# Sparse attention and a gated MLP in one kernel: the scores of the first chunk between its transposes, small copies moved between engines, and one unit's output transposed on TensorE

## The chip, the cores and the metric

The kernel runs on one core of a Trainium2 chip. It is one program with five instruction queues: TensorE (PE, its weight loads shown apart as PEld), VectorE (DVE), ScalarE (ACT), GpSimd (POOL) and SyncE (SP, which here only issues DMAs). The engines work through their own queues in order and wait for each other by semaphores. The metric is the device time of one execution in microseconds (us); lower is better.

## The reference

Attention with 4 batches, 8 heads, 768 positions and a head width of 64, all in float32, then an MLP. Heads 0, 2 and 6 are full causal heads ("retrieval"); the other five see only the first 4 positions and a window of 64.

```python
scores = scale * q @ k.transpose(0, 1, 3, 2)
causal = rel >= 0                          # rel = query position - key position
stream = causal & ((pos_k < n_sink) | (rel < window))     # n_sink 4, window 64
a = softmax(where(causal if retrieval[head] else stream, scores, -1e9))
x = (a @ v).transpose(0, 2, 1, 3).reshape(3072, 512)      # heads side by side
h = x @ w_in                               # w_in 512 x 2048
out = (h * sigmoid(beta * h)) @ w_out      # w_out 2048 x 512
```

## The kernel before, in words

**Units and chunks.** The work is cut into 32 units. A unit is one pair of heads for one half (384 rows) of one batch; four units make a chunk (384 rows of all 8 heads), and there are 8 chunks. Units 0 to 3 are chunk 0 (batch 0, first half), units 4 to 7 chunk 1 (batch 1, first half), units 8 to 11 chunk 2 (batch 0, second half), and so on.

**Steps of a unit.** `steps_T` transposes keys and queries on TensorE (line 350), the results are copied out of PSUM to `KT` (VectorE, line 351) and to the two halves of `QTD` (line 356). `sinks_of` makes `KO` on GpSimd: a copy of the key blocks with the sink columns put in (lines 333 and 334). `steps_QK` multiplies (line 415), for units below 8 adds the mask by a second matmul (line 421), and ScalarE takes the exponential into `es` (line 424). The scores of a unit come in three or more fills; a fill that holds a window block with sinks reads `KO`. `values` casts v into `VX` (`cast_v`, line 275) and copies the masked blocks into `VO` on GpSimd (lines 285 and 286). `steps_PV` multiplies into `po` (line 459), and VectorE normalises into `x` (lines 462 and 464). `x` is transposed into `xT` either on TensorE (`steps_X`, line 491, copied out of PSUM at line 493) or by a DMA (`x_by_dma`, line 475, from SP's queue; units 8 to 29).

**The MLP.** `steps_G1` is a product of four matmuls with `w_in` (line 510), a tanh on ScalarE (line 513) and the gate on VectorE (line 516): 16 such groups for a chunk, which need all four `xT` of the chunk. `steps_G2` is the product with `w_out` (line 534), copied out by ScalarE (line 538) and stored. These groups fill TensorE between the attention steps.

**Loads.** For chunks 0 to 2, q and k come as float32 by SP (`load_qk`, line 119: two pairs of heads at a time) and are cast to bfloat16 into `qkb` by `cast` (line 269; the engine is chosen by the caller); v comes by SP too (`load_v`, line 132). `held=True` puts a small memset on GpSimd ahead of the load, so that the load is issued only when GpSimd's queue gets there. `load_w_in` (line 140) and `load_w_out` (line 144) are DMAs from GpSimd's queue that cast on the way. From chunk 3 on the rows of q and k are loaded and cast by GpSimd's DMAs (lines 303 and 308) into the former staging buffers (`rows_queries` clears one of them first, a memset of 128 x 1536, line 232), and DMA transposes on SP's queue make `KT` (line 319) and `QTD` (line 322).

**The order.** The order on every engine is the order of the calls in the program. The part for chunks 0 and 1 (lines 653 to 736, the "ramp" here) is written out by hand. From unit 8 on, a loop over slots `t` lays scores of unit t, values of unit t - 1 and a fixed number of MLP groups beside each other; `later(delay, f)` places work of the other engines by a running estimate of TensorE's time. PSUM holds two buffers for transposes (`tp`), two for scores (`sp`), three shared ones (`mm`) and one for `po`.

Of the kernel before, what the change touches and what calls it, by code (L numbers as in the profile page):

```python
# [17 lines left out]
def kernel(  # L18
# [13 lines left out]
    nc = tc.nc  # L32
# [66 lines left out]
    st_u = {}  # L99
# [23 lines left out]
    def load_v(c, held=False, tiles=range(HT)):  # L123
        b, h2 = chunks[c]
        if tiles[0] == 0:
            staged["v", c] = stage.tile([128, HT, H, D], F32, name="vs")
        vs = staged["v", c]
        if held:
            nc.gpsimd.memset(vs[:, :, 0, 0:1], 0.0)
        for t in tiles:  # L130
            r = h2 * HALF + t * 128
            nc.sync.dma_start(out=vs[:, t], in_=v[b, :, r:r + 128, :].rearrange("h p d -> p h d"))
# [5 lines left out]
    def load_w_in(i):  # L138
        f = slice(i * 512, (i + 1) * 512)
        nc.gpsimd.dma_start(out=w_in_sb[:, :, f], in_=moe_w_in.rearrange("(mo mi) f -> mi mo f", mi=128)[:, :, f])  # L140
# [54 lines left out]
    def negatives():  # L195
        nc.vector.tensor_scalar(out=Mc, in0=Nc, scalar1=0.0, scalar2=None, op0=ALU.is_ge)
        for i, m in enumerate([M0, Mo, Md, Mo, Md]):
            nc.vector.tensor_scalar(out=Ns[:, i * 128:(i + 1) * 128], in0=m, scalar1=-1.0, scalar2=-NEG, op0=ALU.add, op1=ALU.mult)
# [72 lines left out]
    def cast_v(u):  # L271
        b, h2, p = units[u]
        c = u // NPAIR
        copy = nc.scalar.copy if u in (1, 3) else nc.vector.tensor_copy if 8 <= u < 16 else nc.gpsimd.tensor_copy
        copy(out=VX[b % 2, p][:, h2 * HT:(h2 + 1) * HT, :, 0:D], in_=staged["v", c][:, :, 2 * p:2 * p + 2, :])  # L275

    def values(u):
# [64 lines left out]
    def steps_T(u):  # L342
        b, h2, p = units[u]
        s = st_u.setdefault(u, {})

        def go():
            tk, tq = tile_t(), tile_t()
            for i, tp in ((1, tk), (0, tq)):
                for t in range(HT):
                    nc.tensor.transpose(tp[:, t, :], s["qkb"][:, i, t].rearrange("p h d -> p (h d)"), ident)  # L350
            nc.vector.tensor_copy(out=KT[b % 2, p][:, h2 * HALF:(h2 + 1) * HALF].rearrange("p (j t) -> p j t", t=HT),  # L351
                                  in_=tk.rearrange("p t j -> p j t"))
            s["QT"] = QT = QTB[u % 3]
            for hh in range(2):
                copy = nc.vector.tensor_copy if hh and u not in (1, 4) else nc.scalar.copy
                copy(out=QT[hh][half(hh), :].rearrange("p (j t) -> p j t", t=HT),  # L356
                     in_=tq[half(hh)].rearrange("p t j -> p j t"))

            if u >= 8:
                s["values"] = later(1500, lambda: values(u))  # L360
            s["sinks"] = later(600, lambda: sinks_of(u))
        return [(350, go)]
# [79 lines left out]
    def steps_PV(u):  # L442
        b, h2, p = units[u]
        s = st_u.setdefault(u, {})

        def head(hh, qi, last):
            def go():
                for f in s["masks"] + [s["values"]]:
                    f()
                if "po" not in s:  # L450
                    if u < 8 and u % 2:
                        po = ps_m.tile([128, 512], F32, name="mm") if u < 4 else ps_s.tile([128, 512], F32, name="sp")
                        s["po"] = po[:, 0:HT * 2 * (D + 1)].rearrange("p (t h d) -> p t h d", t=HT, h=2)
                    else:
                        s["po"] = ps_o.tile([128, HT, 2, D + 1], F32, name="po")
                po = s["po"]
                lst = s["blocks"][hh][qi]
                for j, (e, val) in enumerate(lst):
                    nc.tensor.matmul(po[:, qi, hh, :], e, val, start=(j == 0), stop=(j == len(lst) - 1))  # L459
                if last:  # L460
                    rec = att.tile([128, HT, 2, 1], F32, name="rec")
                    nc.vector.reciprocal(rec, po[:, :, :, D:D + 1])
                    x = att.tile([128, HT, 2, D], BF16, name="x")
                    nc.vector.tensor_mul(x, po[:, :, :, 0:D], rec.to_broadcast([128, HT, 2, D]))  # L464
                    s["x"] = x
                    if 8 <= u < NU - 2:
                        later(700, lambda: x_by_dma(u))
            return (len(s["blocks"][hh][qi]) * 38, go)
        return [head(hh, qi, hh == 1 and qi == HT - 1) for qi in range(HT) for hh in range(2)]
# [11 lines left out]
    def steps_X(u):  # L481
        b, h2, p = units[u]
        s = st_u.setdefault(u, {})

        def go():
            c = u // NPAIR
            if c not in xT:
                xT[c] = moe.tile([128, MO, HALF], BF16, name="xT", bufs=3)
            tp = tile_t()
            for t in range(HT):  # L490
                nc.tensor.transpose(tp[:, t, :], s["x"][:, t].rearrange("p h d -> p (h d)"), ident)
            copy = nc.scalar.copy if u < 8 else nc.vector.tensor_copy
            copy(out=xT[c][:, p, :], in_=tp.rearrange("p t j -> p (t j)"))
            avail.add((c, p))
            since[c] = clock[0]
            del st_u[u]
        return [(170, go)]
# [125 lines left out]
    def transposes_of(u):  # L623
        step(steps_T(u)[0])

    def run(steps):
        for x in steps:
            step(x)
# [19 lines left out]
    def cast_dp(u):  # L648
        cast(u, "k", dve)
        cast(u, "q")  # L650


    cast_dp(0)
    load_v(0, held=True)
    transposes_of(0)
    cast_dp(1)
    transposes_of(1)
    negatives()
    st_u[0]["sinks"]()
    st_u[1]["sinks"]()  # L660
    load_w_in(0)
    load_qk(1, 0, held=True)
    cast_dp(2)
    cast_dp(3)
    run(steps_QK(0))
    transposes_of(2)
    run(steps_QK(1))
    transposes_of(3)
    run(steps_QK(2))
    run(steps_QK(3))  # L670
    st_u[2]["sinks"]()
    load_qk(1, 1, held=True)
    rows_queries(1, "s1")
    st_u[3]["sinks"]()
    load_v(1, held=True)
    step((100, beta_go))
    for u in range(4):
        values(u)
    cast(4, "kq", nc.scalar.copy)
    cast(5, "q")  # L680
    load_w_in(1)

# [7 lines left out]
    cast(5, "k", dve)  # L690
    qk = steps_QK(4)
    step(qk[0])
    run(steps_PV(3))
    step(qk[1])
    step(steps_X(2)[0])
    transposes_of(5)
    step(qk[2])
    step(steps_X(3)[0])
    load_w_in(2)
    cast_dp(6)  # L700
    run(steps_QK(5))
    ms(1)
    transposes_of(6)
    ms(1)
    cast_dp(7)
    run(steps_QK(6))
    load_w_in(3)
    transposes_of(7)
    ms(1)
    run(steps_QK(7))  # L710
    ms(1)
    for u in range(4, 8):
        st_u[u]["sinks"]()
    values(4)
    values(5)
    load_w_out(0)
    load_w_out(1)
    values(6)
# [35 lines left out]
    for t in range(8, NU + 2):  # L754
        if t == 8:
            cast_dp(9)
        if t + 2 < 12:
            cast_dp(t + 2)
        if t == 11:
            rows_queries(0, "s0")  # L760
        if t == 12:
            masks_late(0)

        if t < 11:
            some = rows3[6:] if t == 8 else []
        elif t < 14:
            some = load_rows(4)[3 * (t - 11):3 * (t - 10)]
        else:
            c = (t + 6) // NPAIR
            i = (t + 6) % NPAIR  # L770
            some = load_rows(c)[i * 2 + (i > 1):i * 2 + 2 + (i > 0)] if c < NCHUNK else []
        for i, f in enumerate(some):
            later(1000 + 1500 * i, f)
        c, i = (t + 4) // NPAIR, (t + 4) % NPAIR
        if t >= 12 and c < NCHUNK and i < HT:
            later(2500, lambda c=c, i=i: load_v(c, tiles=[i]))
        if t == 9:
            transposes_dma(3, "k")
        if t == 10:
            transposes_dma(3, "q")  # L780
        if t >= 14 and t % NPAIR == 2 and t // NPAIR + 1 < NCHUNK:
            transposes_dma(t // NPAIR + 1)
        if 12 <= t + 1 < NU:
            sinks_at(t + 1, 1000)
            values_at(t + 1, 3000)
        qk = steps_QK(t) if t < NU else []
        pv = steps_PV(t - 1) if 8 <= t - 1 < NU else []
        xx = steps_X(t - 2) if t >= NU else []
        tr = steps_T(t + 1) if t + 1 < 12 else []

        A = qk[:2] + xx
        qk = qk[2:]
        n = max(len(qk), len(pv))
        for i in range(n):
            A += pv[i:i + 1] + qk[i:i + 1] + (tr if i == 0 else [])
        nm = nm_of.get(t, 7)
        if t >= NU:
            ms(3)
            nm -= 3
        slot(A, nm)  # L800
# [41 lines left out]
```

## Time and profile before

| | us |
|---|---|
| median of 3 runs (lowest, highest) | 245.78 (244.87, 248.98) |
| the profiled execution, its own time | 245.14 |
| its span, first to last instruction | 243.4 |
| PE busy | 228.4 (94%) |
| DVE / ACT / POOL busy | 147.3 / 160.9 / 102.8 |
| bytes moved by DMA | 33.85 MB |

The profiled execution lies 0.64 us under the median. Its span leaves out 1.74 us around the first and last instruction. A row of the timeline gives start, duration, engine, line, operation and what it writes and reads; a row of the waits gives who waited for whom, total, times and longest, all in us. A DMA row in the list of issues ends with the time from issue to landing. In the row of the windows the number behind the engines' columns is the granted clock of TensorE, 1.00 being full speed. Matmuls are pipelined, so durations of neighbours overlap; distances between starts are the better measure there.

### The profile page before, as it was taken

How to read it: one execution, taken by the hardware profiler on the slowest of the kernel's cores; microseconds unless marked ns; L12 is line 12 of the kernel's file. 1: busy time of each engine (PE TensorE's matmuls, PEld its weight loads, DVE VectorE, ACT ScalarE, POOL GpSimd, SP SyncE). 2: the span in 40 equal slices, each digit the busy share in tenths (PEclk: the TensorE clock that was granted, in tenths of full speed). 3: DMA queues.
4: the chain of work that ended last, by engine and by line, in shares of the span. 5: the costliest groups of instructions: out<-in, count | busy, mean ns of one | idle time of the engine just before them, and what ended most of it. 6: DMA issues, size and time to landing. Idle time of an engine off the chain costs nothing.

```text
span 243.4 us, 5238 instructions
## 1 busy us (share of the span) xinstructions
PE 228.4 (94%) x1901; PEld 138.4 (57%) x1901; DVE 147.3 (61%) x379; ACT 160.9 (66%) x312; POOL 102.8 (42%) x247
## 2 busy tenths in 40 slices
PE   7687999999999979799999999999999999999993
PEld 3476665555565656556655666566655666455541
DVE  4747668885787559855774577447762766345400
ACT  2598877875757769746775568667884877256510
POOL 6667399011839964297228823950380000000000
PEclk9799999999999999999999999999999999999999
DMA  6999989999989999999989996989421100201112
GB/s 205 192 280 221 180 133 207 213 157 251 189 171 155 183 184 170 153 110 163 147 197 125 168 197 139 147 163 148 103 62 59 60 18 0 79 10 46 43 46 86
DMA packets 103658, 33.85 MB, mean 139 GB/s; under 512 B 90304, under 2 KB 100560, under 8 KB 103632
## 3 DMA queue, kind: packets, MB, share of 16 engines
q1 hardware_dynamic: 67392, 24.98, 49.0%
q0 software_dynamic: 35664, 8.13, 38.7%
q10 hardware_dynamic: 576, 0.40, 0.5%
q8 instruction: 15, 0.25, 0.4%
q14 instruction: 11, 0.09, 0.1%
HBM read 27.27 MB, written 6.29 MB: 138 GB/s over the span
## 4 chain that ended last, share of the span: by engine, by line
PE 79%; ACT 5%; DVE 5%; DMA 4%; POOL 4%; issue 2%; POOLq 0%; ACTq 0%
PE mm L510 30%; PE tp L534 25%; PE sp L415 8%; PE mm L534 7%; PE po L459 4%; ACT es L424 2%; DMA QTD<-s 2%; DMA xT<-x 2%; PE mm L167 2%; DVE gT L516 1%; PE tp L350 1%; ACT QTD L356 1%; DVE x L464 1%; POOL VX L275 1%; ACT osb L538 1%
## 5 line engine op out<-in xcount | busy, mean ns | idle before, releaser
L510 PE MATMUL mm<-xT,w_in_sb 128*128 128x384 bf16 x512 | 98.1, 326 | 1.7 <-DMA xT<-x 1.4
L513 ACT ACTIVATE th<-mm,beta_h 128x384 f32<-128x384 f32 x128 | 74.5, 582 | 27.2 <-PE mm L510 22.5
L516 DVE SCALAR_TENSOR_TENSOR gT<-th,mm 128x384 bf16<-128x384 f32 x128 | 69.8, 551 | 31.0 <-ACT th L513 28.0
L534 PE MATMUL tp<-w_out_sb,gT 128*128 128x512 bf16 x288 | 70.7, 379 | 0.5 <-ACT osb L538 0.5
L510 PEld LDWEIGHTS <-w_in_sb 128*128 128x128 bf16 x512 | 46.2, 97 | 26.3 <-issue 1.6
L534 PEld LDWEIGHTS <-gT 128*128 128x128 bf16 x384 | 34.9, 98 | 30.7 <-issue 0.6
L415 PE MATMUL sp<-QTD,KT 128*128 128x128 bf16 (+2 forms) x261 | 46.4, 244 | 2.7 <-DMA QTD<-s 1.3
L424 ACT ACTIVATE esL<-sp 128x384 bf16<-128x384 f32 x72 | 37.7, 542 | 15.3 <-PE sp L415 15.1
L424 ACT ACTIVATE es<-sp 128x512 bf16<-128x512 f32 (+1 forms) x56 | 30.8, 561 | 7.5 <-PE sp L415 6.9
L415 PEld LDWEIGHTS <-KT 128*128 128x128 bf16 x272 | 25.1, 99 | 12.9 <-issue 4.2
L534 PE MATMUL mm<-w_out_sb,gT 128*128 128x512 bf16 x96 | 24.1, 379 | 0.0
L275 POOL CAST VX<-vs 128x384 bf16<-128x384 f32 x22 | 11.3, 516 | 30.2 <-issue 16.1
L308 POOL DMA_DIRECT2D s<-in_q_dram x30 | 22.3, 751 | 2.2 <-issue 1.7
L333 POOL COPY KO<-KT 128x128 bf16<-128x128 bf16 (+1 forms) x32 | 13.0, 406 | 22.3 <-DVE KT L351 17.2
L538 ACT ACTIVATE osb<-tp 128x512 f32<-128x512 f32 x18 | 10.8, 597 | 14.7 <-PE tp L534 14.4
L459 PEld LDWEIGHTS <-es 128*128 128x128 bf16 x220 | 14.1, 98 | 8.9 <-issue 1.5
L459 PEld LDWEIGHTS <-esL 128*128 128x128 bf16 x252 | 14.7, 98 | 7.7 <-DVE x L464 0.5
L431 DVE TENSOR_TENSOR es<-es,Mh 128x512 bf16<-128x512 bf16 (+2 forms) x30 | 12.9, 431 | 8.3 <-ACT es L424 8.2
L436 DVE TENSOR_TENSOR esL<-esL,Mc 128x128 bf16<-128x128 bf16 x36 | 9.1, 252 | 12.2 <-ACT esL L424 12.2
L459 PE MATMUL po<-VX,esL 128*128 128x65 bf16 x216 | 16.3, 193 | 0.1
L464 DVE TENSOR_TENSOR x<-po,rec 128x384 bf16<-128x384 f32 x28 | 15.6, 557 | 1.0
L415 PE MATMUL sp<-QTD,KO 128*128 128x128 bf16 x79 | 14.8, 220 | 0.0
(85 smaller groups left out, 214.8 us busy)
## 6 DMA issues: line engine op xcount, KB each, us to landing
vs<-in_v_dram SPq DMA_DIRECT2D x24, 256.0 KB, 5.0
out_dram<-osb SPq DMA_DIRECT2D x24, 256.0 KB, 2.5
w_in_sb<-in_moe_w_in_dram POOLq DMA_DIRECT2D x4, 512.0 KB, 5.9
w_out_sb<-in_moe_w_out_dram POOLq DMA_DIRECT2D x4, 512.0 KB, 9.0
s<-in_k_dram SPq DMA_DIRECT2D x5, 384.0 KB, 5.9
s<-in_q_dram SPq DMA_DIRECT2D x5, 384.0 KB, 6.7
s<-in_k_dram POOLq DMA_DIRECT2D x15, 128.0 KB, 5.6
s<-in_q_dram POOLq DMA_DIRECT2D x30, 64.0 KB, 4.0
```

The lines of the kernel that those rows point to most:

```text
L275: copy(out=VX[b % 2, p][:, h2 * HT:(h2 + 1) * HT, :, 0:D], in_=staged["v", c][:, :, 2 * p:2 * p + 2, :])
L308: nc.gpsimd.dma_start(out=ROWS[c % 2, "q"][:, t, :, 3 * D * hh:3 * D * hh + D], in_=q[b, hh:H:2, r:r + 128, :].rearrange("h p d -> p h d"))
L333: nc.gpsimd.tensor_copy(out=ko[:, ka - 1:kz - 1, :], in_=kt[:, ka * 128:kz * 128].rearrange("p (a j) -> p a j", a=n))
L415: nc.tensor.matmul(sp[:, (i - lo) * 128:(j - lo) * 128], lst[i][1], s["QT"][lst[i][0]][:, q0 * 128:(q0 + j - i) * 128], start=True, stop=n ...
L424: nc.scalar.activation(out=es[:, lo * 128:hi * 128], in_=sp[:, 0:w], func=ACTF.Exp, scale=scale)
L459: nc.tensor.matmul(po[:, qi, hh, :], e, val, start=(j == 0), stop=(j == len(lst) - 1))
L464: nc.vector.tensor_mul(x, po[:, :, :, 0:D], rec.to_broadcast([128, HT, 2, D]))
L510: nc.tensor.matmul(hp[:, 0:HALF], w_in_sb[:, mo, fi * 128:(fi + 1) * 128], xT[c][:, mo, :], start=(mo == 0), stop=(mo == MO - 1))
L513: nc.scalar.activation(out=th, in_=hp[:, 0:HALF], func=ACTF.Tanh, scale=beta_h[:, fi:fi + 1])
L516: nc.vector.scalar_tensor_tensor(out=gTs[c][:, fi, :], in0=th, scalar=1.0, in1=hp[:, 0:HALF], op0=ALU.add, op1=ALU.mult)
L534: nc.tensor.matmul(op, gTs[c][:, fi, ns * 128:(ns + 1) * 128], w_out_sb[:, fi, :], start=(fi == 0), stop=(fi == FO - 1))
L538: nc.scalar.activation(out=osb, in_=op, func=ACTF.Copy, scale=0.5)
```

## The change

- **Ramp, chunk 0.** The first fill of a unit's scores is put ahead of the transposes of the next unit (before, both transposes of units 0 and 1 came first and then whole units of scores). `negatives()` (six small VectorE operations that make the additive masks) goes ahead of the first `KT` copy. k of unit 1 is cast on ScalarE instead of VectorE. `load_qk(1, 1)` is released right behind `load_qk(1, 0)`.
- **Copies.** `VX` of units 1 and 3 goes from ScalarE to VectorE, one `QTD` half of unit 1 from ScalarE to VectorE, `xT` of units 0 and 1 from ScalarE to VectorE. q and k of unit 4 were both cast on ScalarE; now k is cast on VectorE between the two `VX` copies and q on GpSimd between `values(1)` and `values(2)`.
- **GpSimd's queue.** The casts of units 6 and 7 are split and drawn forward. `values(4)`, the load of the last quarter of `w_in`, `values(5)` and the memset of `rows_queries(1, "s1")` move from behind the scores of unit 7 (and, the memset, from ahead of v of chunk 1) to directly behind the scores of unit 5, and so ahead of `KO` of unit 6.
- **Unit 11.** Its `x` is transposed on TensorE in slot 13 instead of by DMA. The DMA transposes of the keys of chunk 4 are issued at slot 13 instead of 14, those of its queries at slot 14 as before, and the row loads for chunks 3 and 4 are placed closer together.

```diff
-        copy = nc.scalar.copy if u in (1, 3) else nc.vector.tensor_copy if 8 <= u < 16 else nc.gpsimd.tensor_copy
+        copy = nc.vector.tensor_copy if u in (1, 3) or 8 <= u < 16 else nc.gpsimd.tensor_copy
...
-                copy = nc.vector.tensor_copy if hh and u not in (1, 4) else nc.scalar.copy
+                copy = nc.vector.tensor_copy if hh and u != 4 else nc.scalar.copy
...
-                    if 8 <= u < NU - 2:
+                    if 8 <= u < NU - 2 and u != 11:
                         later(700, lambda: x_by_dma(u))
...
-            copy = nc.scalar.copy if u < 8 else nc.vector.tensor_copy
+            copy = nc.scalar.copy if 2 <= u < 8 else nc.vector.tensor_copy
...
     cast_dp(0)
     load_v(0, held=True)
+    negatives()
     transposes_of(0)
-    cast_dp(1)
+    st_u[0]["sinks"]()
+    cast(1, "k", act)
+    cast(1, "q")
+    qk = steps_QK(0)
+    step(qk[0])
     transposes_of(1)
-    negatives()
-    st_u[0]["sinks"]()
+    step(qk[1])
+    step(qk[2])
     st_u[1]["sinks"]()
+    cast_dp(2)
     load_w_in(0)
     load_qk(1, 0, held=True)
-    cast_dp(2)
+    load_qk(1, 1, held=True)
     cast_dp(3)
-    run(steps_QK(0))
+    qk = steps_QK(1)
+    step(qk[0])
     transposes_of(2)
-    run(steps_QK(1))
+    step(qk[1])
+    step(qk[2])
+    qk = steps_QK(2)
+    step(qk[0])
     transposes_of(3)
-    run(steps_QK(2))
+    step(qk[1])
+    step(qk[2])
     run(steps_QK(3))
     st_u[2]["sinks"]()
-    load_qk(1, 1, held=True)
-    rows_queries(1, "s1")
     st_u[3]["sinks"]()
     load_v(1, held=True)
     step((100, beta_go))
-    for u in range(4):
-        values(u)
-    cast(4, "kq", nc.scalar.copy)
+    values(0)
+    values(1)
+    cast_dp(4)
+    values(2)
+    values(3)
     cast(5, "q")
     load_w_in(1)
...
     step(qk[0])
+    cast(6, "q")
+    load_w_in(2)
     run(steps_PV(3))
...
-    load_w_in(2)
-    cast_dp(6)
+    cast(7, "q")
+    cast(6, "k", dve)
     run(steps_QK(5))
+    values(4)
+    load_w_in(3)
+    values(5)
+    rows_queries(1, "s1")
     ms(1)
     transposes_of(6)
     ms(1)
-    cast_dp(7)
+    cast(7, "k", dve)
     run(steps_QK(6))
-    load_w_in(3)
...
-    values(4)
-    values(5)
     load_w_out(0)
...
-        if t < 11:
-            some = rows3[6:] if t == 8 else []
-        elif t < 14:
-            some = load_rows(4)[3 * (t - 11):3 * (t - 10)]
+        if t < 14:
+            some = rows3[6:] if t == 8 else load_rows(4)[3 * (t - 11):3 * (t - 10)] if t > 10 else []
...
-            later(1000 + 1500 * i, f)
+            later((1000 if t != 13 else 200) + (1500 if t > 13 else 1000) * i, f)
...
+        if t == 13:
+            transposes_dma(4, "k")
+        if t == 14:
+            transposes_dma(4, "q")
-        if t >= 14 and t % NPAIR == 2 and t // NPAIR + 1 < NCHUNK:
+        if t > 14 and t % NPAIR == 2 and t // NPAIR + 1 < NCHUNK:
             transposes_dma(t // NPAIR + 1)
...
-        xx = steps_X(t - 2) if t >= NU else []
+        xx = steps_X(t - 2) if t == 13 or t >= NU else []
```

More of the change, by code (lines that the diff above doesn't have):

```diff
@@ L650, in cast_dp @@
         cast(u, "q")
+    act = nc.scalar.copy
     cast_dp(0)
     load_v(0, held=True)
+    negatives()
     transposes_of(0)
-    cast_dp(1)
+    st_u[0]["sinks"]()
[3 more added lines that the diff above has]
+    step(qk[0])
     transposes_of(1)
-    negatives()
-    st_u[0]["sinks"]()
+    step(qk[1])
+    step(qk[2])
     st_u[1]["sinks"]()
+    cast_dp(2)
     load_w_in(0)
     load_qk(1, 0, held=True)
-    cast_dp(2)
+    load_qk(1, 1, held=True)
     cast_dp(3)
-    run(steps_QK(0))
+    qk = steps_QK(1)
+    step(qk[0])
     transposes_of(2)
-    run(steps_QK(1))
+    step(qk[1])
+    step(qk[2])
+    qk = steps_QK(2)
+    step(qk[0])
     transposes_of(3)
-    run(steps_QK(2))
+    step(qk[1])
+    step(qk[2])
     run(steps_QK(3))
     st_u[2]["sinks"]()
-    load_qk(1, 1, held=True)
-    rows_queries(1, "s1")
     st_u[3]["sinks"]()
```

## The prediction

> **What bounds the kernel now.** I read the page first, then what TensorE waits for.
>
> ```profile
> span 243.4 us, 5238 instructions
> ...
> PE   7687999999999979799999999999999999999993
> ...
> PEclk9799999999999999999999999999999999999999
> ...
> PE 79%; ACT 5%; DVE 5%; DMA 4%; POOL 4%; issue 2%; POOLq 0%; ACTq 0%
> ```
>
> TensorE is nine tenths busy from slice 6 on, so whatever comes late there moves the end, and work hidden elsewhere does not. Its idle time is in the first six slices (0 to 37 us) and in slices 14 and 16. The waits of TensorE over the whole span name the two later holes:
>
> ```profile
> PE tp L350 <- DVE qkb L269: 1.7, 1, 1.7
> PE mm L510 <- DMA xT<-x: 1.4, 1, 1.4
> ...
> PE sp L415 <- DMA QTD<-s: 1.3, 1, 1.3
> ```
>
> The second row is unit 11's x by DMA (issued at 82.61, landed 4.67 later; TensorE stood to 87.32), the third the queries of chunk 4 (TensorE stood to 99.85). Behind 101 us it has no DMA wait.
>
> In the ramp no single engine bounds. Up to 16.65 it is ScalarE, then hand-overs between all of them. The rows that matter for this change, from the timeline:
>
> ```profile
> 10.51 0.37 SPq L119 DMA_DIRECT2D s<-in_k_dram  x1
> 10.97 0.45 SPq L119 DMA_DIRECT2D s<-in_q_dram  x1
> ...
> 17.34 0.20 DVE L462 RECIPROCAL rec<-po 128x6 f32<-128x6 f32 x1 [0.86 <-PE po L459]
> 17.46 0.95 ACT L269 CAST qkb<-s 128x384 bf16<-128x384 f32 x2
> 17.73 0.50 POOL L275 CAST VX<-vs 128x384 bf16<-128x384 f32 x1
> ```
>
> and, from the DMA view of the stretch in which these two loads are issued, the time to landing:
>
> ```profile
> s<-in_k_dram SPq DMA_DIRECT2D x1, 384.0 KB, 5.8
> s<-in_q_dram SPq DMA_DIRECT2D x1, 384.0 KB, 6.5
> ```
>
> So k of chunk 1 lands at 16.3 and q at 17.5. Before, ScalarE cast them at 17.46, when it was free anyway: nobody waited.
>
> **Part 1: slots 12 to 16.** The x DMA of unit 11 goes; its wait is 1.45 in TensorE's timeline. Three transposes come in at 0.055 each (spacing of such rows at full clock): +0.17. They need x (VectorE, done at 82.6) and stand behind the first fills of slot 13, at about 82.8; the copy (0.55) finds VectorE idle for 1.26 at 83.4, so xT is there by 83.9 against a use at 85.4. Hidden; without that cover it would cost up to 0.55. The keys' three DMA transposes (4.5 on SP) move ahead of one v load and one store, and x's 1.2 leave SP; the queries start about when the store is out, 86.4 instead of 91.2. The row loads they need are drawn forward on GpSimd by some 2 (before, the last landed at 91.6), so the third query transpose goes out at about 89.5 and lands 5.3 later, 94.8, against a use at 97.3. The wait of 1.27 goes, with 2.5 to spare. What stands behind the transposes on SP are a store and loads that have several us. What is late next is nothing in the trace: TensorE is dense behind it. Sum -1.45 + 0.17 - 1.27 = **-2.55**; bounds 0 (both waits come back in other form) to -2.7.
>
> **Part 2: the start, 6 to 16.** I laid the changed order out with these durations. Scores of unit 0 start at 6.8 instead of 8.3; ScalarE has 5.3 of exponentials plus three query copies and one cast from 6.7, and ends at about 14.5 instead of 16.8: 2.3 earlier. The masks (0.75) lie in VectorE's idle time before 6.08. But GpSimd still casts q of unit 2 when it lands (9.03), and then issues w_in and the memsets that release the next loads, at 10.5 as before. So the 16.3 and 17.5 stay. Now VectorE has beta, VX of unit 1, **k of unit 4**, VX of unit 3, then the reciprocal of unit 0. k waits to 16.3; 0.5 for it and 0.47 for VX give a reciprocal at 17.35, against 17.34. GpSimd holds VX and VO of unit 2 behind q, to 17.5; they end at 19.2, as before. The gain of 2.3 is given back whole. Taken: **0**; bounds -2.0 (both have landed) and +0.3.
>
> **Part 3: 17 to 27.** VectorE now carries xT of units 0 and 1 (0.5 each in these rows). The second half of the transposes of unit 4 needs the PSUM buffer that xT of unit 0 empties: 19.4 instead of 19.1; the keys' copy of unit 5 stands 1.0 later, but its queries wait for ScalarE as before. Scores of unit 5 start at 23.55 instead of 23.24: +0.3. A further cost is the clock. The windows of 3.41 in which the granted clock changes:
>
> ```profile
> 5.90:9.31 3.41, 1.53 (x20) 1.16 (x19) 2.64 (x8) 1.25 (x3) 1.22 (x5) 1.00 1.10 260
> 9.31:12.72 3.41, 3.02 (x26) 2.36 (x24) 2.33 (x7) 2.55 (x6) 2.50 (x8) 0.50 0.76 128
> ```
>
> A window with TensorE busy 1.53 of 3.41 was followed by one at 0.50; the window 16.13 to 19.55, busy 2.35, was followed by full clock. In the changed order TensorE has done values of units 0 and 1 by 15.2 and stands to 18.2, so that window holds some 0.8. The next one, with 2.44 of work before, then runs at half clock: between 0 (its gaps take it) and 2.4, taken 0.8. The Trainium skill, "TensorE: Matmul & The Clock Gate", Part 1, says that the clock is halved after a whole idle window of about 3.4 us; by that rule, with 0.8 us of work in the window, this term is 0 and the sum is 0.8 lower. The row above speaks against it, half a window of work was not enough, so I keep the 0.8.
>
> **Part 4: GpSimd's queue, 23 to 36.** KO of unit 6 is needed by its second fill:
>
> ```profile
> 14.58 1.38 POOL L232 MEMSET s<- 128x1536 bf16 x1
> ...
> 26.60 0.29 POOL L333 COPY KO<-KT 128x128 bf16<-128x128 bf16 x1 [3.39 <-DVE KT L351]
> ...
> 29.99 0.51 POOL L275 CAST VX<-vs 128x384 bf16<-128x384 f32 x1
> ```
>
> Before, GpSimd was idle for 3.39 ahead of it. In the changed order VX and VO of unit 4 (1.04), w_in (0.74), VX and VO of unit 5 (1.04) and the memset (1.38) stand there: 4.2 behind KO of unit 5 (24.2 with the half clock), so KO of unit 6 ends at 28.9 and its fill starts then instead of at 27.19: **+1.7**, which contains the 1.1 of part 3. Behind it stand KO of unit 7, w_out, and v of units 6 and 7. What the move takes away from 30 to 36 comes back: from 27.19 to the dense groups (37.33) before were 10.1, of them about 0.9 in which TensorE stood for VO and x. Net of the ramp: **+0.8**, bounds -0.5 and +1.7, if v of chunk 1 has landed by 24.
>
> It need not have. Its third load is in the DMA view
>
> ```profile
> vs<-in_v_dram SPq DMA_DIRECT2D x1, 256.0 KB, 10.6
> ```
>
> issued at 19.0, landed at 29.65. SP took 2.1 to push it, until 21.1, while w_in (19.8) got in first: between 22.5 and 24.5 the DMA view shows 398 packets of GpSimd's queue and 23 of SP's. Released 3 us earlier (12.7), it is still held by the full queue, until 19.7 to 20.6 by my count of packets; w_in goes out at 20.05. It should be ahead on most rings and land at 24, if not at 26.
>
> **The sum.** 245.14 (the profiled execution's own time; the median of the runs is 0.64 higher) - 2.55 + 0.8 = **243.4 us**, 0.7% less. 2% (4.9 us) is about what a measurement of this kernel can tell from no change.
>
> **Rivals.**
> - *v of chunk 1 lands at 26* (its last rings behind w_in). KO of unit 6 at 30.9, dense groups +2.9: 245.5. For it: the order of issue is close to a tie.
> - *Slower: GpSimd stands at VX of unit 4 as long as v took before.* If v lands behind the second w_in too, at 29.65 plus the 0.8 by which that w_in is later, KO of unit 6 ends at 35.1, its fill is 7.9 late, 9.2 of TensorE's work remain to the dense groups (+7.0), and the hole of 8 puts a window at half clock behind it (+0.9): 245.14 - 2.55 + 7.9 = 250.5. It decides from a landing at about 29.5 on. For it: that is exactly the landing before, and the same two w_in loads are in flight. Against: its push ends up to 1.4 earlier, w_in's second issue is 0.8 later.
> - *The early gain holds.* If q and k of unit 4 have landed when VectorE and GpSimd get there, x of unit 0 is at 16.2, TensorE keeps its clock, and up to 2.0 stay: 240.6, down to 239.5. Against: 12.0 to 14.0 shows 367 packets of w_in alone while these loads, issued at 10.5, stand. The Trainium skill, "DMA: Bandwidth & Descriptors", section on queues, rings and completion order, says that a DMA engine takes turns between its queues; by that the loads would land about 1 us sooner and the sum be about 1 lower. Those 367 packets do not show it.
> - *The change does not do what it says in slots 12 to 16*: the queries still land late, because the row loads don't come earlier. 1.3 to 2.5 of part 1 stay: 245.3.
>
> **Chances.** Forecast 0.40 (242 to 244.8); v at 26 0.16; slower rival 0.24 (248.5 to 252.5, nearly all of it over the 2% bound); early gain 0.14 (239.5 to 241.5, three quarters of it within 2%); queries late 0.06. So faster 0.04 from the early rival and 0.06 for gains I don't see, 0.10; slower 0.22; within 2% 0.68. The range takes in the early rival's middle and the lower part of the slower one: 240.4 to 249.8, about 0.2 left out.
>
> **What would show it.** Right: no waits of L510 for xT or of L415 for QTD near 85 and 98; VectorE's cast of k (L269) waits for the DMA to about 16.3 and the first reciprocal stays near 17.3; L415 waits for KO near 28; granted clock 0.5 near 20 to 23. Wrong: the reciprocal of unit 0 before 16.5; KO of unit 6 by 27.2 or after 33; a DMA wait behind 101.

## The result and the profile after

| | before | after |
|---|---|---|
| median of 20 runs each (lowest, highest) | 245.45 (244.2, 248.98) | **249.48** (245.91, 254.8) |
| ratio, with its 95% interval | | **1.0114** (1.0078 to 1.0149) |
| profiled execution, its span | 245.14, 243.4 | 249.17, 247.5 |

By the ratio the changed kernel is 1.1% slower. That is within 2% of no change, to which the prediction gave 0.68, but on the other side of it than the 243.4 forecast. The ratios here and below leave out runs more than 1.5% above the fastest of the same kernel and the medians do not, so a kernel whose runs spread widely looks worse by its median (1.6% here) than by its ratio. The runs of the changed kernel spread over 8.9 us where those before spread over 4.8; the lowest and highest spans go with the granted clock (244.2 at a mean of 0.985, 253.0 at 0.958).

The page of the changed kernel: span, TensorE and its clock in 40 slices, and the chain that ended last by engine:

```profile
span 247.5 us, 5215 instructions
...
PE   7768589999999999699999999999999999999993
...
PEclk9985979999999999999999999999999999999998
...
PE 77%; DMA 9%; DVE 5%; POOL 3%; SPq 2%; ACT 2%; issue 1%; ACTq 0%; POOLq 0%
```

The ramp now has two stretches of lowered clock (slices 3 and 5, counted from 0) and a thin slice 4, and of the two later holes one is left, in slice 16. DMA has risen from 4% to 9% of the chain. What TensorE waited for, over the whole span (total, times, longest):

```profile
PE sp L415 <- POOL KO L334: 3.1, 1, 3.1
PE sp L415 <- DMA QTD<-s: 2.6, 2, 2.2
PE tp L491 <- DVE x L464: 2.1, 2, 2.0
```

The wait for x of unit 11 (1.4) is gone. The wait for the queries of chunk 4 has grown from 1.3 to 2.2 in one piece, and a wait of 3.1 for `KO` of unit 6 is new.

**Two marks** split the time from here on. M1 is the start of the 41st matmul of L510 (in the dense groups, all waits of the ramp behind it), M2 that of the 201st (behind slot 16 and the queries of chunk 4). Before: M1 39.09, M1 to M2 73.07, the rest 131.26. After: 43.67, 72.72, 131.07. So the ramp lost 4.58 where 0.8 was forecast, and slots 12 to 16 gained 0.35 where 2.55 was forecast.

**The ramp.** Rows of the timeline of the changed kernel:

```profile
16.04 0.55 DVE L269 CAST qkb<-s 128x384 bf16<-128x384 f32 x1 [1.06 <-DMA s<-in_k_dram]
...
16.97 0.18 DVE L462 RECIPROCAL rec<-po 128x6 f32<-128x6 f32 x1
17.29 0.50 POOL L269 CAST qkb<-s 128x384 bf16<-128x384 f32 x1 [1.73 <-DMA s<-in_q_dram]
...
19.82 0.74 POOL L140 DMA_DIRECT2D w_in_sb<-in_moe_w_in_dram  x1
...
26.86 0.51 POOL L275 CAST VX<-vs 128x384 bf16<-128x384 f32 x1 [3.13 <-DMA vs<-in_v_dram]
...
29.69 1.37 POOL L232 MEMSET s<- 128x1536 bf16 x1
31.01 0.28 POOL L333 COPY KO<-KT 128x128 bf16<-128x128 bf16 x1
...
31.59 0.29 PE L415 MATMUL sp<-QTD,KO 128*128 128x128 bf16 x1 [3.14 <-POOL KO L334]
```

VectorE and GpSimd stand for k and q of unit 4, as forecast. GpSimd then stands 3.13 for v of chunk 1, whose third load landed at 26.80, and `KO` of unit 6 comes out at 31.54. The windows of 3.41 there (width, busy time of the five engines, granted clock of TensorE, DMA share, GB/s):

```profile
13.79:17.20 3.41, 1.58 (x29) 1.14 (x26) 1.78 (x6) 1.01 (x3) 0.63 (x3) 1.00 1.12 335
17.20:20.62 3.42, 2.68 (x29) 2.35 (x30) 2.75 (x8) 0.94 (x2) 3.14 (x9) 0.50 1.21 278
20.62:24.03 3.41, 3.00 (x33) 2.77 (x31) 1.95 (x6) 1.93 (x4) 2.57 (x7) 0.50 0.97 141
...
27.45:30.86 3.41, 0.96 (x9) 0.49 (x7) 2.37 (x5) 1.52 (x4) 3.22 (x7) 1.00 0.76 112
30.86:34.27 3.41, 2.68 (x22) 2.41 (x23) 0.56 (x1) 1.36 (x3) 0.64 (x4) 0.50 0.65 107
```

Both thin windows (1.58 and 0.96 of TensorE's work) are followed by half clock. The first is the term of Part 3. The second is a consequence of the hole at `KO`, and had a price only in the slower rival.

### The profile page after: what moved, and what is told of

Same layout as the page of the kernel before. It is cut to its first block, busy times and chain, and to the rows that moved or that the text cites. A ratio compares the mean times of both kernels' runs of the same rounds, so it can differ in the third digit from the quotient of the medians.

```text
span 247.5 us, 5215 instructions
## 1 busy us (share of the span) xinstructions
PE 228.8 (92%) x1879; PEld 140.8 (57%) x1904; DVE 151.2 (61%) x385; ACT 158.4 (64%) x306; POOL 103.7 (42%) x248
## 4 chain that ended last, share of the span: by engine, by line
PE 77%; DMA 9%; DVE 5%; POOL 3%; SPq 2%; ACT 2%; issue 1%; ACTq 0%; POOLq 0%
PE mm L510 28%; PE tp L534 24%; PE sp L415 9%; PE mm L534 8%; DMA QTD<-s 5%; PE po L459 4%; DMA vs<-in_v_dram 3%; PE mm L167 2%; SPq L132 2%; PE tp L350 1%; DVE gT L516 1%; DVE x L464 1%; ACT osb L538 1%; POOL VX L275 1%; PE sp L421 1%
## 5 line engine op out<-in xcount | busy, mean ns | idle before, releaser
L510 PE MATMUL mm<-xT,w_in_sb 128*128 128x384 bf16 x512 | 98.2, 326 | 0.4 <-DVE gT L516 0.2
L534 PE MATMUL tp<-w_out_sb,gT 128*128 128x512 bf16 x269 | 67.1, 379 | 1.4 <-ACT osb L538 0.5
L510 PEld LDWEIGHTS <-w_in_sb 128*128 128x128 bf16 x512 | 46.4, 98 | 26.5 <-issue 1.9
L424 ACT ACTIVATE esL<-sp 128x384 bf16<-128x384 f32 x72 | 37.8, 542 | 15.4 <-PE sp L415 15.3
L534 PE MATMUL mm<-w_out_sb,gT 128*128 128x512 bf16 x90 | 23.2, 379 | 0.2
L333 POOL COPY KO<-KT 128x128 bf16<-128x128 bf16 (+1 forms) x32 | 13.0, 405 | 24.0 <-DVE KT L351 18.1
L459 PEld LDWEIGHTS <-es 128*128 128x128 bf16 x220 | 14.5, 101 | 8.2 <-issue 0.8
L431 DVE TENSOR_TENSOR es<-es,Mh 128x512 bf16<-128x512 bf16 (+2 forms) x30 | 12.2, 408 | 8.0 <-ACT es L424 7.9
L459 PE MATMUL po<-VX,esL 128*128 128x65 bf16 x216 | 16.3, 193 | 0.1
```

The costliest lines, as they stand in the source:

```text
L333: nc.gpsimd.tensor_copy(out=ko[:, ka - 1:kz - 1, :], in_=kt[:, ka * 128:kz * 128].rearrange("p (a j) -> p a j", a=n))
L424: nc.scalar.activation(out=es[:, lo * 128:hi * 128], in_=sp[:, 0:w], func=ACTF.Exp, scale=scale)
L510: nc.tensor.matmul(hp[:, 0:HALF], w_in_sb[:, mo, fi * 128:(fi + 1) * 128], xT[c][:, mo, :], start=(mo == 0), stop=(mo == MO - 1))
L534: nc.tensor.matmul(op, gTs[c][:, fi, ns * 128:(ns + 1) * 128], w_out_sb[:, fi, :], start=(fi == 0), stop=(fi == FO - 1))
```

## The experiments

Each run was timed beside the kernel before on the same chip. M1, M1 to M2 and the third query transpose of chunk 4 (issued, landed) are from each profiled run.

| run | ratio to before (95%) | M1 | M1 to M2 | third query transpose |
|---|---|---|---|---|
| before | 1 | 39.09 | 73.07 | 94.40, 99.72 |
| after | 1.011 (1.008, 1.015) | 43.67 | 72.72 | 97.05, 103.85 |
| slots alone | 1.013 (1.004, 1.022) | 38.76 | 76.03 | 92.03, 100.60 |
| unit 11 alone | 0.998 (0.994, 1.002) | 39.86 | 74.88 | 95.14, 100.62 |
| slots, rows of chunk 4 earlier | 1.005 (1.000, 1.010) | 38.83 | 73.64 | 95.17, 99.93 |
| slots, rows of chunk 5 late | 0.999 (0.995, 1.003) | 38.77 | 70.58 | 91.87, 96.43 |
| slots, rows of 5 to 7 held | **0.984** (0.979, 0.988) | 39.23 | 70.48 | 92.40, 96.55 |
| rows held alone | 0.990 (0.987, 0.994) | 39.37 | 71.78 | 94.86, 98.72 |
| ramp alone | 1.004 (0.999, 1.009) | 40.74 | 72.91 | 96.44, 101.22 |
| after, `KO` first | 1.015 (1.006, 1.023) | 40.42 | 74.49 | 93.49, 100.71 |
| after, unit 4 on ScalarE | 1.033 (1.027, 1.040) | 44.50 | 77.62 | 98.61, 106.90 |
| after, both | 1.014 (1.005, 1.023) | 41.05 | 78.30 | 96.35, 104.27 |
| after, w_in later | 1.006 (1.002, 1.009) | 39.50 | 77.51 | 93.45, 101.63 |
| after, w_in later, fill | 1.011 (1.008, 1.014) | 39.82 | 72.97 | 92.92, 100.25 |
| after, rows held | 0.991 (0.988, 0.995) | 40.81 | 70.52 | 94.81, 98.22 |
| after, all three | 0.991 (0.987, 0.994) | 40.90 | 70.33 | 94.05, 97.49 |

The rest behind M2 was 130.5 to 132.2 in all of them but one, which is told below.

### Pieces of the ramp undone on the changed kernel

```diff
     run(steps_QK(5))
-    values(4)
-    load_w_in(3)
-    values(5)
-    rows_queries(1, "s1")
     ms(1)
...
```

(Units 4 and 5 of v go back behind `KO` of units 6 and 7, and the load behind `KO` of unit 6, where they were. The memset goes behind the loads of `w_out`, later than it ever stood.)

> The changed kernel with the GpSimd block put back: values(4), the last quarter of w_in, values(5) and the memset of 128 x 1536 stand behind KO of units 6 and 7 again. Theory A (GpSimd's queue stands for v of chunk 1, and KO of unit 6 stands behind it): TensorE's wait of 3.1 us for KO goes, and so does the half-clock window behind it (0.9): 3.5 to 4.2 us less than the changed kernel, within 1 us of the kernel before. Theory B (the copies moved to VectorE and the half clock at 17 to 24 us carry the loss): within 1 us of the changed kernel, 2 to 3 us above the one before.

Median 249.52 (247.15 to 252.32). The `KO` wait is gone and M1 is 3.25 earlier than in the changed kernel, although v landed at 27.36: nobody on the path waits for it any more. So theory A had the wait right, but not the time, which stayed where theory B put it: M1 to M2 is 1.77 longer. TensorE came earlier to the queries of chunk 4, stood 2.28 there, and 101.64 to 105.05 ran at half clock. Taking the `KO` wait out gave no faster kernel.

```diff
     values(1)
-    cast_dp(4)
     values(2)
     values(3)
+    cast(4, "kq", nc.scalar.copy)
```

> The changed kernel with q and k of unit 4 both cast on ScalarE behind values(3), as before; all else as changed. x of unit 0 then need not wait for the load of k: done by 16.3 instead of 17.75, and the hole of TensorE at 15.8 to 17.8 shrinks by 1 or more. Theory A (KO of unit 6 is set by the landing of v at 26.8, whatever comes earlier): KO of unit 6 still ends near 31.5 and the time stays within 0.7 us of the changed kernel. Theory B (hole and half clock carry the loss): 2 us or more below the changed kernel.

Median 253.04, the slowest of all. v landed at 26.75 and `KO` of unit 6 ended at 31.50, as theory A had it, but the time is neither theory's. TensorE now stood 2.7 for the casts of unit 4 on ScalarE and still 2.7 for `KO`, and M1 came 0.83 later than in the changed kernel. The larger part of the loss is behind M1: 4.4 at the queries, with 105.86 to 112.69 at half clock. So the new place of these two casts is not what makes the ramp late; the other copies were not tried one by one.

> Both edits at once: GpSimd block back, q and k of unit 4 on ScalarE. Theory A: the gain of 2.3 us on ScalarE is no longer given back at the reciprocal, and nothing waits for v; the dense groups start 0.5 to 1.5 us before those of the kernel before (39.1), and with the 0.4 us from slots 12 to 16 the time is 1 to 2 us below the kernel before. Theory B: no lower than the better of the two single edits.

Median 249.64. M1 41.05 without a wait for `KO`, then 5.1 at the queries of chunk 4, with 102.92 to 109.75 at half clock. In all three, M1 to M2 is longer than in the changed kernel, by 1.77 to 5.58: a loss lies behind M1 too.

### The slot part alone

```diff
-                    if 8 <= u < NU - 2:
+                    if 8 <= u < NU - 2 and u != 11:
...
+        if t == 13:
+            transposes_dma(4, "k")
...
```

(All of the change from slot 11 on, on the old ramp.)

> The kernel before with the slot part alone: unit 11 transposed on TensorE, keys of chunk 4 at slot 13, row loads closer together. If the slots give what the profile of the changed kernel shows (wait for xT gone, wait for the queries 0.9 longer): 0.3 to 0.5 us below the kernel before. If the forecast holds and only the late ramp spoilt it (both waits gone): 2.5 us below.

Median 247.31 against 244.85, slower by 1.3% in the ratio, where both expectations had it faster. The part from which all of the gain was to come is a loss by itself. Its timeline at the queries of chunk 4, and the windows around that hole:

```profile
100.84 0.32 PE L415 MATMUL sp<-QTD,KT 128*128 128x384 bf16 x1 [3.86 <-DMA xT<-x]
```

```profile
98.70:102.11 3.41, 1.27 (x10) 0.89 (x11) 0.26 (x2) 0.75 (x2) 0.01 (x1) 1.00 1.50 206
102.11:105.52 3.41, 3.41 (x24) 2.09 (x23) 2.00 (x6) 2.42 (x5) 3.17 (x8) 0.50 0.67 82
```

(The wait is for several semaphores; the row names x, but the last thing this matmul reads, the third query transpose, landed at 100.60.) The sum closes: 73.07, less the two old waits of 2.72, plus 0.17 of transposes, the hole of 3.86 and 1.7 for the half clock in one window is 76.08; measured 76.03.

Why did the transpose land 0.9 later though it was issued 2.4 earlier? It took 8.6 instead of 5.3. The DMA view of the slot part alone, of the single microsecond 98 to 99:

```profile
DMA packets 1227, 0.16 MB, mean 155 GB/s; under 512 B 1227, under 2 KB 1227, under 8 KB 1227
## 3 DMA queue, kind: packets, MB, share of 16 engines
q0 software_dynamic: 1227, 0.16, 243.3%
```

Only packets of GpSimd's queue start in it, some 128 bytes each, and their times add up to 2.4 times what 16 engines have in a microsecond. They are the rows of k and q for chunk 5, issued at 86.98, 88.67, 92.17 and 93.90; all four loads overlap the flight of the third query transpose (92.03 to 100.60). In the kernel before, three overlap its flight (94.40 to 99.72), one of them only to 94.54; there the same microsecond has 644 packets of SyncE's queue beside 383 of GpSimd's. The change moved the query transposes forward and left these loads nearly where they were (the last two go out 1.6 earlier), so the transposes came to lie further among them. Over the 16 profiled runs the third query transpose of chunk 4 took 3.4 to 4.6 with no row load of chunk 5 in flight beside it (five runs), 4.8 to 5.5 with two or three (four runs) and 6.8 to 8.6 with four (seven runs, the changed kernel among them).

### Unit 11 alone, and rows of chunk 4 earlier

```diff
-        xx = steps_X(t - 2) if t >= NU else []
+        xx = steps_X(t - 2) if t == 13 or t >= NU else []
...
```

(With the condition on unit 11 at its DMA, and with no DMA of chunk 4 moved.)

> The kernel before with only unit 11's x on TensorE; no DMA transpose of chunk 4 and no row load is moved. Theory (the queries of chunk 4 land when the DMA engines let them, at about 99.7 as before): the wait for x (1.3 us) goes, TensorE comes 1.3 earlier to the queries and stands 2.5 there instead of 1.3; no gain, 245 us, and 1.7 more (246.7) if that hole puts one window of 3.41 at half clock. Rival (as predicted, a hole removed is time gained): the query wait stays 1.3 and the time is 243.6.

Median 245.5 against 246.14, no difference. As the theory had it, the wait for x goes (1.45) and the one for the queries grows, to 2.94 with half clock behind it.

```diff
-        if t == 11:
+        if t == 10:
             rows_queries(0, "s0")
...
-            some = rows3[6:] if t == 8 else load_rows(4)[3 * (t - 11):3 * (t - 10)] if t > 10 else []
+            some = rows3[6:] if t == 8 else load_rows(4)[3 * (t - 10):3 * (t - 9)] if 9 < t < 13 else []
```

> The kernel before with the change's part in slots 12 to 16, and the row loads of chunk 4 issued one slot earlier than the change has them (slots 10 to 12). Theory (the moved transposes stand behind other transfers, not behind their rows): the third query transpose still lands after 98.5, TensorE stands 1.5 us or more there, 245 to 247.5. Rival (my prediction's step, only aimed too late: the rows were what they waited for): the third lands by 96.5, no wait for the queries, 242.4.

Median 248.67, ratio 1.005. The same collision appears one chunk earlier: the rows of chunk 4 now run beside the query transposes of chunk 3, whose third lands 8.4 after its issue (the profiled execution, 245.3, is the fastest of its ten). At chunk 4 the rows had landed by 84.87, and yet the third query transpose went out only at 95.17, behind the keys' transposes, a v load, a store and the first two query transposes on SyncE's queue; so the rows were not all that it waited for. The row of the timeline at the queries of chunk 3:

```profile
80.34 0.32 PE L415 MATMUL sp<-QTD,KT 128*128 128x384 bf16 x1 [3.43 <-DMA QTD<-s]
```

Earlier is not enough; the loads must not lie beside the transposes of any chunk.

### The rows of the next chunks held back

```diff
             some = load_rows(c)[i * 2 + (i > 1):i * 2 + 2 + (i > 0)] if c < NCHUNK else []
+            if t < 17:
+                some = load_rows(c)[:7] if t == 16 else []
...
```

(Chunk 5 alone, on top of the slot part. The seven loads of slot 16 are placed 0.7 apart instead of 1.5.)

> The kernel before with the change's part in slots 12 to 16, and the five row loads of chunk 5 that GpSimd issues in slots 14 and 15 held back to slot 16. Theory (these loads take the DMA engines that the query transposes of chunk 4 need; between 98 and 99 of the run of the slot part alone only their packets moved): third query transpose lands by 97.8, hole at most 0.5, no half clock behind it, 242.3 to 243.5. Rival (SyncE's own pushing of the transposes is what takes long): third lands after 99, hole of 2 or more, 246 to 247.5. A new wait for the queries of chunk 5 near 120 would show that the loads were held back too long.

The mechanism is confirmed: with nothing changed but the row loads of chunk 5 moved, the third query transpose of chunk 4 lands at 96.43 instead of 100.60, TensorE does not wait, and M1 to M2 is 70.58. But the expected time was missed (246.18 against 246.14): TensorE came earlier to the queries of chunk 5, which now lie beside the rows of chunk 6, and stood 3.49 there, with two windows at half clock behind it. The rest behind M2 is 137.09. Holding the rows of all later chunks is the next step:

```diff
-            some = load_rows(c)[i * 2 + (i > 1):i * 2 + 2 + (i > 0)] if c < NCHUNK else []
+            some = {0: slice(0, 5), 1: slice(5, 9)}.get(t % NPAIR, slice(0, 0))
+            some = load_rows(c)[some] if c < NCHUNK else []
...
-            later((1000 if t != 13 else 200) + (1500 if t > 13 else 1000) * i, f)
+            later((1000 if t != 13 else 200) + (900 if t > 13 else 1000) * i, f)
```

> The kernel before with the change's part in slots 12 to 16, and the row loads of chunks 5 to 7 moved from the four slots ahead of their DMA transposes to the last two of these, so behind the query transposes of the chunk before. Theory (row loads of the next chunk and query transposes share the DMA engines, and the former make the latter late): third query transposes of chunk 4 by 97 and of chunk 5 by 120.5, no query wait over 0.5 on TensorE, 242 to 243.5, faster than both kernels. Rival (the DMA engines have no room there in any order): the keys' transposes of chunk 5 wait for their rows, a wait of 2 or more near 110 or 122, 245.5 to 248.

Median **241.79** (240.97 to 242.7) against 245.48: ratio 0.984, faster than both kernels and just under the time expected. The page, and the same transpose in the DMA view:

```profile
span 240.2 us, 5214 instructions
...
PE   7687999999999999999999999999999999999993
...
PEclk9799999999999999999999999999999999999999
```

```profile
QTD<-s SPq DMA_TRANSPOSE x1, 4.2
```

Slice 16 is full, no DMA wait of TensorE is left, and the landing takes 4.2 where the slot part alone took 8.6. M1 to M2 is 2.59 shorter than before.

> The kernel before with only the row loads of chunks 5 to 7 held back as in the run at 241.79; x of unit 11 and the transposes of chunk 4 stay as before. Theory (the slot part's own gain is x's wait and an earlier start of the query transposes, and it is the row loads that kept it from the time): the x wait of 1.3 stays, the third query transpose starts near 94 and lands by 98.5 to 99, a query wait of 0 to 1 is left, 243.5 to 244.5. Rival (the held loads are the whole gain and the change's part in slots 12 to 16 is worth nothing): 241.5 to 242.5.

Median 243.09 against 245.66. Holding the rows is worth 1.0% without the change: it takes away the hole at the queries (M1 to M2 -1.29), and the x wait stays. The time lies between the two expectations, nearer the first. The row of the timeline at x of unit 11:

```profile
87.52 0.32 PE L510 MATMUL mm<-xT,w_in_sb 128*128 128x384 bf16 x1 [1.42 <-DMA xT<-x]
```

The change's slot part adds 1.30 more in the traces (71.78 to 70.48) and about 0.7% in the ratios. Together the two are worth 2.59, about the 2.55 that was forecast for the slot part; by itself, beside held loads, the slot part is worth half of that.

### What the ramp costs

> The changed ramp with the old slots 12 to 16. Theory (the two parts add as they do in the trace of the changed kernel: dense groups 4.6 later, slots 0.4 better): 249.5 to 250.2, with the KO wait of about 3 near 31, the x wait of 1.3 and the query wait of 1.3 both back. Rival (most of the loss is the slot part, as the run of it alone, 1.3% slower, suggests; the ramp part's lateness is taken up later): 246 to 247.5.

Median 248.04 against 246.14, ratio 1.004 with an interval that includes 1; M1 at 40.74, neither of the two expectations. Here q of unit 4 landed at 18.55, 1.4 later than in the changed kernel, GpSimd came 1.4 later to the load of `w_in`, and v landed before it, at 24.20. GpSimd's rows in this run have no wait for v:

```profile
21.20 0.74 POOL L140 DMA_DIRECT2D w_in_sb<-in_moe_w_in_dram  x1
...
24.65 0.51 POOL L275 CAST VX<-vs 128x384 bf16<-128x384 f32 x1
```

What comes first, the issue of w_in or the end of SyncE's push of v (the row that issues the third v load: 2.3 long in the changed kernel, to 20.68), looks like a switch. To force it:

```diff
     cast(5, "q")
-    load_w_in(1)
...
     cast(6, "q")
+    load_w_in(1)
     load_w_in(2)
```

> The changed kernel with the load of the second w_in quarter issued beside the third's, behind q of unit 6, so some 1.7 us later (at about 21.5, where SyncE's push of the third v load ends at 20.7). Theory (the lateness of GpSimd in the profiled run of the changed kernel is the tie of these two loads: with w_in at 19.8 and v's push open until 20.7, v landed at 26.8; in the run of the changed ramp alone w_in went out at 21.2 and v landed at 24.2): v lands by 24.5, no KO wait of 3, dense groups at 40.5 to 41.5 instead of 43.7, and 1.5 to 2.5 less than the changed kernel: about 247. Rival (v's landing does not depend on that order): v at 26 to 27, KO wait of 3, about 249.5.

v landed at 23.89, and GpSimd hardly waited for it, by the timeline of this run:

```profile
23.94 0.51 POOL L275 CAST VX<-vs 128x384 bf16<-128x384 f32 x1 [0.16 <-DMA vs<-in_v_dram]
```

All nine profiled runs with the changed ramp fit this: in the four with w_in issued before that push ended v landed at 26.0 to 27.4, in the five with w_in behind it at 23.9 to 24.8. The `KO` wait fell to 1.1 and M1 to 39.50, 4.2 earlier than in the changed kernel. The median is 247.3. By the ratios about 0.6% (1.4 us) came through; the profiled execution (249.24, so above the median) shows where the rest can go: a hole of 4.1 at the queries and two windows at half clock.

```diff
     run(steps_PV(1))
+    idle(8, ps_s, "sp")
     step(steps_X(0)[0])
```

(Matmuls of zeros; w_in is later here too.)

> As the run with the later w_in, and eight matmuls of zeros (128x512, results unused) on TensorE between the values of unit 1 and the transposes of x of unit 0, where it stands for 2 us. Theory (that standing sets off the half clock that follows): full clock from 17 to 27, scores of unit 5 some 1 to 2 earlier, time 0.5 to 1.5 below the run without them. Rival (the half clock comes from the thin work behind it): half clock as before, time the same or up to 1 more.

The fill did what it was to do: no window at half clock from 17 us to the last few. It gave no time: M1 39.82 against 39.50, median 249.0 against 247.3. TensorE reaches `KO` of unit 6 earlier and stands 2.1 there instead of 1.1; GpSimd's queue sets that point, not the clock. From the waits of this run:

```profile
PE sp L415 <- POOL KO L334: 2.1, 1, 2.1
```

> The changed kernel with the row loads of chunks 5 to 7 held back, nothing else. Theory (its ramp costs what the dense groups' start shows, 4.6 in the profiled run where v of chunk 1 landed at 26.8, 1 to 2 where it lands by 24.5, and nothing of it is taken up behind): 244 to 246.5 by the median, no query wait over 0.5, and more by 2 to 4.5 than the same on the old ramp. Rival (the changed ramp by itself costs nothing, as the lateness is taken up by later waits): 241.5 to 243.

Median 244.01, ratio 0.991. Neither DMA transposes nor `KO` hold TensorE for more than 0.4; the wait that is left is 3.0 for x of unit 0. In this run q of unit 4 landed late again (cast at 19.29) and v at 24.81; M1 is 40.81, 1.6 behind the same slots on the old ramp, and the ratios differ by 0.8%. So the changed ramp costs about 1.6 to 1.9 with the rows held, and none of it is taken up behind. The theory had 2 to 4.5 for it.

> The changed kernel with all three edits: w_in later, the matmuls of zeros, and the held row loads. Theory (the losses add and each has its cause): no KO wait, no query wait over 0.5, dense groups near 40, the time of the held row loads on the old ramp (242 to 243.5) plus 0 to 1.5: 242.5 to 244.5. Rival (the changed ramp has a loss of its own that none of these takes away): 245 to 247.

Median 243.48, ratio 0.991: the time is the first theory's, but the `KO` wait that it ruled out is there, and it is no better than held rows alone on this ramp. What remains is GpSimd's queue ahead of `KO` (a wait of 2.2, and a window at half clock behind it from 29.77).

## Why the prediction was right and wrong

**Part 1 (slots), wrong in one step.** The step is "the third query transpose goes out at about 89.5 and lands 5.3 later, 94.8". In the changed kernel it went out at 97.05 and landed 6.8 later; in the slot part alone, without the late ramp, it went out at 92.03 and landed 8.6 later. The first half fails there because the last rows of chunk 4 were issued 1.3 earlier, not 2, and landed only 0.3 earlier (91.38 against 91.64), and because SyncE was busy pushing the second transpose until 91.85. The second half fails because the 5.3 was taken over from a stretch with fewer row loads of chunk 5 in flight beside the transpose, and in the new stretch there were four. I had counted the DMAs that move and the queues they move past, but not those that stay and share the 16 engines. "What is late next is nothing in the trace" and the bound of 0 fell with it: the stretch lost 2.96. The sum of the two waits was right: with the rows held, M1 to M2 shrank by 2.49 to 2.74 in four runs, against 2.55. But 1.29 of it comes by holding the rows alone.

**Part 2 (start), right.** ScalarE's exponentials end at 14.80 (forecast 14.5), k is waited for to 16.04 (16.3), and the reciprocal of unit 0 stands at 16.97 (17.35; before 17.34). Of the 2.3 us, 0.4 is left there.

**Part 3 (17 to 27), right in size.** The half clock came (17.20 to 24.03), and the transposed keys of unit 6 were copied 1.15 later than before (27.13 against 25.98); 0.3 + 0.8 was forecast. By the Trainium skill, "TensorE: Matmul & The Clock Gate", Part 1, a whole idle window halves the clock; the window ahead of it had 1.58 of work in 3.41, so the trace speaks against that rule. But with the fill the clock stayed full and no time came back: this term was not on the path once GpSimd is late.

**Part 4 (GpSimd's queue), mechanism right, landing wrong.** The step is "it should be ahead on most rings and land at 24". In the profiled run v landed at 26.80, and the rival "v at 26" happened; its `KO` at 30.9 was measured at 31.54. Its price was too small: 2.9 forecast, 4.58 measured at M1. Of the missing 1.7, 0.6 is the later `KO`. The rest, about 1.0, fits the half clock in the window behind the 3.14 hole, which I had priced in the slower rival only: its 2.68 of TensorE's work would take 1.34 at full clock. Where v was ahead of w_in (the run with w_in later), `KO` of unit 6 ended at 28.62 against 28.9 forecast, and M1 lies 0.4 behind the profiled run before; 0.8 was forecast, but M1 of the seven profiled runs with the old ramp spreads from 38.76 to 39.86.

**The sum, remade:** 245.14 + 4.58 - 0.35 - 0.19 (behind M2) = 249.18, measured 249.17. Two rivals came true together, "v of chunk 1 lands at 26" and "the queries still land late", and only each by itself had a price; by these prices both would give 245.14 + 2.9 - 2.55 + 2.2 = 247.7. That the stated range, to 249.8, holds the profiled 249.17 and the median of 249.48 is luck: its upper end was put there for the slower rival, with v landing from about 29.5 on, and v landed at 26.80. The 4.58 is one execution, too: M1 was 40.74 and 40.81 in two other profiled runs of the same ramp, 1.7 behind the kernel before. The 2% that the prediction took for the limit of measuring was too wide: with 20 runs each the interval of the ratio is 0.7% wide. The chance of 0.06 for "the queries still land late" was far too low. Its price, "1.3 to 2.5 of part 1 stay", fits this trace, where 2.20 stay, but leaves out that the change can make the queries land later than before: in the slot part alone the stretch lost 2.96 where 2.55 was to be gained.

**Open:** what makes q of unit 4 land at 17.0 to 17.2 in some runs of the changed ramp and at 18.1 to 19.2 in others was not tried. That the wide spread of the changed kernel comes from this tie and from how its holes fall on the clock windows is argued from the traces (the kernel without holes spreads over 1.7 us), not shown.

## What to carry to other kernels

When a DMA is moved earlier, list what every other queue has in flight in the new stretch: the landing is set by the shared engines, and the loads that were not moved must move too. A wait removed ahead of a late transfer only makes the next wait longer, so try a part of a change with the next late thing held off before it is called useless: the slot part was +1.3% by itself and -0.7% beside held loads. And price a hole together with the window of clock behind it.

## What the hardware showed that was not expected

- **The half clock needs no idle window.** Over the profiled runs, from 5 to 235 us, all 18 full-clock windows of 3.41 with at most 1.58 of TensorE's work were followed by half clock. Of those with 1.60 to 2.44, 29 of 32 were followed by full clock; the three others begin between 13.5 and 15.4 us. So more than 1.8 us of standing within one window costs up to another 1.7 in the next, but a hole does so only if one window holds it: the hole of 3.43 at 80 us fell on two windows (1.75 and 1.60 of work) and cost nothing more.
- **Row loads in small packets can leave SyncE's queue nothing.** In the microsecond shown above, 128-byte packets moved 155 GB/s, their times added up to 243% of 16 engines' time, and no packet of SyncE's queue started.
- **Two queues can share by packets, not by bytes.** In the changed kernel, 23 to 25 us, the DMA view shows as many packets of GpSimd's w_in as of SyncE's v, but four times the bytes:

```profile
q0 software_dynamic: 304, 0.31, 90.9%
q1 hardware_dynamic: 307, 0.08, 29.6%
```

The Trainium skill, "DMA: Bandwidth & Descriptors", section on queues, rings and completion order, says that an engine takes turns between its queues by packets; this stretch agrees, as far as the profile's packets are the packets meant there. That this sharing is how w_in, issued 0.9 before the push of v ended, made v late by 2.6 (26.80 against 24.20 in the changed ramp alone) is argued; the runs show that v's landing goes with the order of the two, and that moving w_in behind turned it. In the kernel before, 23 to 24, it was 206 packets to none, so the turns are not always seen.
